# A decode layer on one core: the last 16 columns of wo's last rows as eight small transfers of their own

## The chip, the cores and the metric

The kernel runs on one core of a Trainium2 chip. The core has five engines with queues of their own: TensorE (PE, matmuls and the loads of their weights), VectorE (DVE), ScalarE (ACT), GpSimd (POOL) and SyncE (SP, which issues most transfers). Data move between the chip's main memory (HBM) and the on-chip memory (128 partitions) through 16 transfer (DMA) engines, which all queues share. A transfer is issued by one engine's queue, is cut into packets for the 16 transfer engines, and raises a semaphore when it has landed; whoever needs the data waits until that semaphore has 16.

The metric is the device time of one execution in microseconds (us), lower is better, as the median of several runs.

## What is computed

One token goes through an attention block and a feed-forward block in parallel, and both are added to the input. Cut to what matters:

```python
D, Hq, Hkv, Sk, Dh, F, W = 1024, 32, 4, 65536, 128, 3584, 4096
x  = A_x                                   # 1 x 1024, bf16 as all inputs
xn = layernorm(x)
# attention over the last W = 4096 positions, 8 query heads share a key head
q  = (xn @ wq).reshape(Hq, Dh)             # wq 1024 x 4096
p  = softmax(q . k_cache[:, -W:] * Dh ** -0.5)
o  = p . v_cache[:, -W:]                   # 32 heads x 128 = 4096 numbers
a  = o @ wo                                # wo 4096 x 1024
# feed-forward, with a second layernorm
h  = gelu(layernorm(xn) @ w1 + b1)         # w1 1024 x 3584
b  = h @ w2 + b2                           # w2 3584 x 1024
out = x + a + b
```

Weights and cache together are 40 MB, each byte of which is used once.

## The kernel before

The program is written out by hand, engine by engine; no scheduler reorders it, so the order of each queue is the order of the code.

SP issues all large transfers in one sequence: wq in four pieces (L183), w1 in four (L184), the keys and the values in four pieces each (L185 to L194). Then it waits until the product with w1 is done, since w2 takes w1's place in the on-chip memory and wo takes wq's (tile WA), and issues w2 in four pieces and wo in seven (L285 to L287). The helper `load_rows` (L135) issues such a sequence; its transfers all carry the line L138. At the end SP waits for ScalarE's copy of the result, issues the store of the output (L458) and waits for its landing.

ScalarE issues four small loads at the start: x twice, b2 and b1.

Of wo, partition p holds rows 32p to 32p + 31 of the 4096, one after another, 1024 columns (2 KB) each. So "row c" below means 128 rows of wo, one in each partition, 256 KB in all. `WO_CHUNKS` (L25) says how many of these rows go into each transfer: 8, 8, 8, 4, 2, 1, 1. Each transfer has a semaphore, s_wo0 to s_wo6.

TensorE computes, in this order: the layernorms' sums, the product with wq, the turning of q into columns, the product with w1, the transposes of the keys (L343) with the gelu's part among them, the scores (L365), the softmax's small products, the first chunk of w2, the product with the values (L432), the rest of w2 with the attention output's turning (L443) in between, and at last the seven chunks of wo. The products with w2 and wo are made by `out_rows_mms` (L403): it waits for the chunk's semaphore and then makes four matmuls per row c, one for each quarter of the 1024 output columns. All add into one accumulator. The last matmul raises PE's semaphore, ScalarE copies the result to ORow (L456), and the store follows.

Two things of the code matter for the end of the program: the wo chunks are waited for one by one, in the order of their issue, and the last chunk is a single row c, so that only four matmuls are left when it lands.

Of the kernel before, what the change touches and what calls it, by code (L numbers as in the profile page):

```python
# [9 lines left out]
D = 1024  # L10
# [11 lines left out]
WQ_CHUNKS = [2, 2, 2, 2]  # L22
W1_CHUNKS = [2, 2, 2, 2]
W2_CHUNKS = [9, 9, 8, 2]
WO_CHUNKS = [8, 8, 8, 4, 2, 1, 1]  # L25
PAD = 32


# [12 lines left out]
def bass_parallel_sum__sliding_block_cached__mixer_channel_mlp__decode_kernel(  # L41
# [18 lines left out]
    pe, dve, act, pool, sp = nc.tensor, nc.vector, nc.scalar, nc.gpsimd, nc.sync  # L60

    def sems(name, n):
        return [nc.alloc_semaphore(f"{name}{i}") for i in range(n)]
# [4 lines left out]
    s_k = sems("s_k", HKV)  # L68
    s_v = sems("s_v", HKV)
    s_wo = sems("s_wo", len(WO_CHUNKS))  # L70
    s_w2 = sems("s_w2", len(W2_CHUNKS))

    PE = Track(nc, "S_PE")
# [4 lines left out]
    def sb(name, shape, d):  # L78
        return nc.alloc_sbuf_tensor(name, shape, d)
# [24 lines left out]
    GT = sb("GT", [128, FC + PAD], bf16)  # L104
# [8 lines left out]
    OT = sb("OT", [128, 32 + PAD], bf16)  # L113
# [4 lines left out]
    W2 = W1[:, 0:FC * D]  # L118
    WA = sb("WA", [128, KC * NQ], bf16)
# [10 lines left out]
    wo_p = A_wo.rearrange("(p j) n -> p j n", j=32)  # L130
# [4 lines left out]
    def load_rows(dst, src, chunks, width, semaphores):  # L135
        c0 = 0
        for j, n in enumerate(chunks):
            sp.dma_start(  # L138
                dst[:, c0 * width:(c0 + n) * width].rearrange("p (c n) -> p c n", c=n),
                src[:, c0:c0 + n, :],  # L140
            ).then_inc(semaphores[j], 16)
            c0 += n
# [128 lines left out]
    for h in range(HQ):  # L271
        last = pe.matmul(PSb[:, 7 * 1024 + 2 * h: 7 * 1024 + 2 * h + 1], lhsT=Qrow[0:1, h * 128:(h + 1) * 128],  # L272
                         rhs=identb[0:1, 0:1], is_transpose=True)
# [10 lines left out]

    sp.wait_ge(PE.sem, C["h"])  # L285
    load_rows(W2, w2_p, W2_CHUNKS, D, s_w2)
    load_rows(WA, wo_p, WO_CHUNKS, D, s_wo)  # L287


    KPAIRS = [[0, 1], [2, 3], [4, 5]]  # L290
# [36 lines left out]
    for u in range(NUNIT):  # L327
# [13 lines left out]
        for bb in range(16):  # L341
            o = banks[bb // 8] * 1024 + (bb % 8) * 128
            last = pe.matmul(PSb[:, o:o + 128], lhsT=KT[:, col + bb * 128: col + (bb + 1) * 128],  # L343
                             rhs=identb[:, :], is_transpose=True)
# [16 lines left out]
    for g in range(HKV):  # L361
        if g == HKV - 1:
            wait_kt(pe, 7)
        for b in range(NBLK):
            last = pe.matmul(  # L365
                PS[:, g * 256 + b * 8: g * 256 + (b + 1) * 8],
                lhsT=KT[:, g * W + b * 128: g * W + (b + 1) * 128], rhs=QT[:, g * 8:(g + 1) * 8])
# [32 lines left out]
    def acc(a):  # L400
        return PS[32 * a:32 * a + 32, 6 * 512:6 * 512 + 256]

    def out_rows_mms(weights, vec, chunks, semaphores, j, stop_at=None):  # L403
        c0 = sum(chunks[:j])
        pe.wait_ge(semaphores[j], 16)
        for c in range(c0, c0 + chunks[j]):
            for a in range(4):
                ins = pe.matmul(acc(a), lhsT=vec[:, c:c + 32],  # L408
                                rhs=weights[:, c * D + a * 256: c * D + (a + 1) * 256],
                                start=False, stop=(c == stop_at))  # L410
        return ins
# [4 lines left out]
    for a in range(4):  # L416
        pe.matmul(acc(a), lhsT=identb[0:1, 0:32], rhs=XBR[0:1, a * 256:(a + 1) * 256], start=True, stop=False)
        pe.matmul(acc(a), lhsT=identb[0:1, 0:32], rhs=XBR[0:1, D + a * 256:D + (a + 1) * 256], start=False, stop=False)
    pe.wait_ge(DVE.sem, C["d_GT"])
    out_rows_mms(W2, GT, W2_CHUNKS, s_w2, 0)  # L420
    pe.wait_ge(DVE.sem, C["sump"])
    C["tot"] = PE.mark(pe.matmul(PS[:, 3 * 512:3 * 512 + 1], lhsT=SUMP[:, :], rhs=onesf[:, 0:1]))
    dve.wait_ge(PE.sem, C["tot"])
# [4 lines left out]
    for g in range(HKV):  # L428
        pe.wait_ge(s_v[g], 16)
        for b in range(NBLK):  # L430
            i = g * NBLK + b
            last = pe.matmul(PS[32 * g:32 * g + 32, 4 * 512:4 * 512 + DH],  # L432
                             lhsT=Pb[:, i * REP:i * REP + 32], rhs=V[:, i * DH:(i + 1) * DH],
                             start=(b == 0), stop=(b == NBLK - 1))
# [2 lines left out]
    dve.wait_ge(DVE.sem, C["rec"])  # L437
    C["on"] = DVE.mark(dve.tensor_scalar(out=ON[:, :], in0=PS[:, 4 * 512:4 * 512 + DH], scalar1=REC[:, 0:1],
                                         scalar2=None, op0=ALU.mult))
    out_rows_mms(W2, GT, W2_CHUNKS, s_w2, 1)  # L440
    pe.wait_ge(DVE.sem, C["on"])
    for dq in range(4):
        last = pe.matmul(PS[:, 5 * 512:5 * 512 + 32], lhsT=E4[:, dq * 128:(dq + 1) * 128],  # L443
                         rhs=ON[:, dq * 32:(dq + 1) * 32], start=(dq == 0), stop=(dq == 3))
# [1 line left out]
    dve.wait_ge(PE.sem, C["o2"])  # L446
    C["OT"] = DVE.mark(dve.tensor_copy(OT[:, 0:32], PS[:, 5 * 512:5 * 512 + 32]))
    for j in range(2, len(W2_CHUNKS)):
        out_rows_mms(W2, GT, W2_CHUNKS, s_w2, j)
    pe.wait_ge(DVE.sem, C["OT"])  # L450
    for j in range(len(WO_CHUNKS)):
        last = out_rows_mms(WA, OT, WO_CHUNKS, s_wo, j, stop_at=31)
    C["fin"] = PE.mark(last)

    act.wait_ge(PE.sem, C["fin"])
# [34 lines left out]
```

## Time and profile before

| | |
|---|---|
| median of 3 runs | 102.17 us (101.99 to 102.3) |
| span of the profiled execution, first to last instruction | 100.8 us |
| PE busy, of the span | 69% |
| DVE, ACT, POOL busy | 21%, 14%, 5% |
| read from HBM | 39.86 MB, 395 GB/s over the span |
| DMA packets | 4194, of them 726 under 512 bytes |
| mean granted TensorE clock | 0.823 |

The profile is one execution, taken by the hardware profiler. Its span runs from the program's first to its last instruction. The profiled execution's whole time is not given beside it; the runs' median lies 1.3 to 1.4 us above the span, which is what a launch adds outside of it.

The page's strip divides the span into 40 slices of 2.5 us and gives the busy share of each in tenths. The chain of waits follows the work that ended last back to its beginning. The timeline lists instructions in order of time, alike ones merged, with the idle time before them and what ended it. Windows give the busy times in a chosen stretch; their DMA share is the mean over the 16 transfer engines, so that 1.0 is all sixteen busy (a little over 1 can come up, since packets overlap). The queue table counts packets: q1 is SP's queue, q10 ScalarE's, q8 brings instructions. Every transfer engine that takes part in a transfer has data packets and one 4-byte packet, which raises the semaphore by one.

### The profile page before, as it was taken

Reading aid. Unit: us, or ns where it says so; the run is one execution under the profiler, and the core shown is the slowest. Engines: PE = TensorE matmul, PEld = TensorE weight load, DVE = VectorE, ACT = ScalarE, POOL = GpSimd, SP = SyncE. Lnnn points to the kernel's source line nnn. Section 1 sums busy time; section 2 is a strip of 40 time slices with the busy share of each in tenths; the row PEclk is TensorE's granted clock in tenths of the full one; section 3 lists DMA queues with packets and bytes.
Section 4 is the critical chain, followed back from the end, with each engine's and each line's share of the span. In section 5 each row is a group of like instructions: output and inputs, shape, how many; then the busy total and the mean of one; then the engine's idle time right before and its main releaser. Section 6 shows DMA issues by size and latency. Waiting matters only on the chain.

```text
span 100.8 us, 1803 instructions
## 1 busy us (share of the span) xinstructions
PE 69.3 (69%) x825; PEld 42.7 (42%) x825; DVE 21.4 (21%) x46; ACT 13.8 (14%) x16; POOL 4.8 (5%) x18
## 2 busy tenths in 40 slices
PE   0002399999946999996799984649999934070781
PEld 0001233333304223331799984236999823040420
DVE  0003520000054000002876934555000200000000
ACT  0400060000051000002554740040000000000001
POOL 6740000000000000000000000000000000000000
PEclk9999999999996559999999997555559999555555
DMA  4899999999999999999999999999999999999930
GB/s 104 358 442 432 417 436 416 416 431 427 449 432 392 450 427 404 416 416 426 419 423 423 416 431 456 431 395 443 425 398 447 429 423 435 416 422 403 388 139 1
DMA packets 4194, 39.96 MB, mean 396 GB/s; under 512 B 726, under 2 KB 730, under 8 KB 1244
## 3 DMA queue, kind: packets, MB, share of 16 engines
q1 hardware_dynamic: 3896, 39.85, 94.2%
q8 instruction: 6, 0.10, 0.4%
q10 hardware_dynamic: 292, 0.01, 0.2%
HBM read 39.86 MB, written 0.00 MB: 395 GB/s over the span
## 4 chain that ended last, share of the span: by engine, by line
DMA 38%; PE 34%; SPq 20%; DVE 5%; issue 1%; ACT 1%
PE PS L254 31%; DMA WA<-in_A_wo_dram 30%; SPq L138 20%; DMA XB<-in_A_x_dram 7%; DVE ROW L264 2%; PE PS L272 1%; PE PS L234 1%; PE PS L217 1%; PE PS L408 0%; ACT ORow L456 0%; DVE XNT L225 0%; ACT msx L221 0%; DVE msx L198 0%; DVE msy L198 0%; DVE YT L230 0%
## 5 line engine op out<-in xcount | busy, mean ns | idle before, releaser
L254 PE MATMUL PS<-WA,XNTb 128*1 128x512 bf16 x64 | 16.4, 424 | 0.3 <-DVE msy L198 0.3
L254 PE MATMUL PS<-W,YTb 128*1 128x512 bf16 x56 | 15.0, 438 | 0.0
L408 PE MATMUL PS<-WA,OT 128*32 128x256 bf16 x128 | 7.3, 379 | 9.9 <-DMA WA<-in_A_wo_dram 9.9
L254 PEld LDWEIGHTS PS<-WA,XNTb 128*1 128x1 bf16 x64 | 5.8, 91 | 10.5 <-issue 3.5
L408 PEld LDWEIGHTS PS<-WA,OT 128*32 128x32 bf16 x128 | 3.8, 123 | 13.4 <-DMA WA<-in_A_wo_dram 10.3
L432 PE MATMUL PS<-KV,Pb 128*32 128x128 bf16 x128 | 9.2, 260 | 0.0
L254 PEld LDWEIGHTS PS<-W,YTb 128*1 128x1 bf16 x56 | 5.2, 94 | 9.4 <-issue 4.1
L432 PEld LDWEIGHTS PS<-KV,Pb 128*32 128x32 bf16 x128 | 9.1, 119 | 0.0
L343 PE MATMUL PS<-identb,KV 128*128 128x128 bf16 x128 | 7.5, 219 | 1.5 <-ACT ROW L280 1.5
L343 PEld LDWEIGHTS PS<-identb,KV 128*128 128x128 bf16 x128 | 7.1, 98 | 2.0 <-ACT ROW L280 2.0
L217 PE MATMUL PS<-XT,onesf 128*128 128x16 f32 x2 | 0.6, 384 | 8.7 <-DVE XT L213 8.7
L350 DVE COPY KV<-PS 128x1024 bf16<-128x1024 bf16 x10 | 6.3, 684 | 0.7 <-PE PS L343 0.7
L355 ACT ACTIVATE KV<-PS 128x1024 bf16<-128x1024 bf16 x6 | 5.8, 1018 | 1.9 <-PE PS L343 1.9
L408 PE MATMUL PS<-W,GT 128*32 128x256 bf16 x112 | 4.8, 320 | 1.7 <-DMA W<-in_B_w_dram 1.7
L264 DVE CAST ROW<-PS 1x2048 bf16<-1x2048 f32 x1 | 2.3, 2278 | 15.1 <-PE PS L254 15.1
L282 DVE CAST ROW<-PS 1x2048 bf16<-1x2048 f32 x1 | 2.3, 2279 | 14.8 <-PE PS L254 14.8
L456 ACT ACTIVATE ORow<-PS 128x256 bf16<-128x256 f32 x1 | 0.4, 383 | 31.5 <-PE PS L408 31.5
L408 PEld LDWEIGHTS PS<-W,GT 128*32 128x32 bf16 x112 | 3.5, 111 | 2.5 <-DVE PS L386 2.2
L217 PEld LDWEIGHTS PS<-XT,onesf 128*128 128x128 f32 x2 | 0.5, 310 | 8.7 <-DVE XT L213 8.7
L266 ACT ACTIVATE ROW<-PS 1x2048 bf16<-1x2048 f32 x1 | 1.9, 1866 | 14.1 <-PE PS L254 14.1
L280 ACT ACTIVATE ROW<-PS 1x1536 bf16<-1x1536 f32 x1 | 1.4, 1439 | 16.5 <-PE PS L254 16.5
L365 PE MATMUL PS<-QT,KV 128*128 128x8 bf16 x128 | 3.4, 166 | 0.4 <-DVE KV L350 0.4
(75 smaller groups left out, 34.5 us busy)
## 6 DMA issues: line engine op xcount, KB each, us to landing
WA<-in_A_wq_dram SPq DMA_DIRECT2D x4, 2048.0 KB, 14.1
W<-in_B_w_dram SPq DMA_DIRECT2D x4, 1792.0 KB, 30.6
WA<-in_A_wo_dram SPq DMA_DIRECT2D x3, 2048.0 KB, 38.9
W<-in_B_w_dram SPq DMA_DIRECT2D x2, 2304.0 KB, 22.3
KV<-in_A_k_cache_dram SPq DMA_DIRECT2D x4, 1024.0 KB, 39.4
KV<-in_A_v_cache_dram SPq DMA_DIRECT2D x4, 1024.0 KB, 34.4
W<-in_B_w_dram SPq DMA_DIRECT2D x1, 2048.0 KB, 29.3
WA<-in_A_wo_dram SPq DMA_DIRECT2D x1, 1024.0 KB, 42.2
```

Source lines behind the costliest of these rows:

```text
L138: sp.dma_start(dst[:, c0 * width:(c0 + n) * width].rearrange("p (c n) -> p c n", c=n), src[:, c0:c0 + n, :],).then_inc(semaphores[j], 16)
L217: C["sum1"] = PE.mark(pe.matmul(PS[:, 7 * 512: 7 * 512 + 16], lhsT=onesf[:, :], rhs=XT16[:, 0:16]))
L254: last = pe.matmul(PS[0:1, t * 512:(t + 1) * 512], lhsT=vec[:, k:k + 1], rhs=weights[:, k * width + t * 512: k * width + (t + 1) * 512], s ...
L264: C["d_qrow"] = DVE.mark(dve.tensor_copy(Qrow[:, 0:2048], PS[0:1, 0:2048]))
L266: C["a_qrow"] = ACT.mark(act.activation(out=Qrow[:, 2048:4096], in_=PS[0:1, 2048:4096], func=ACTF.Copy))
L282: C["d_hrow"] = DVE.mark(dve.tensor_copy(Hrow[:, 1536:F], PS[0:1, 1536:F]))
L343: last = pe.matmul(PSb[:, o:o + 128], lhsT=KT[:, col + bb * 128: col + (bb + 1) * 128], rhs=identb[:, :], is_transpose=True)
L350: C["dkt"][u] = DVE.mark(dve.tensor_copy(KT[:, col + 1024 * s: col + 1024 * (s + 1)], PSb[:, bk * 1024:(bk + 1) * 1024]))
L355: C["akt"][u] = ACT.mark(act.activation(out=KT[:, col + 1024: col + 2048], in_=PSb[:, bk * 1024:(bk + 1) * 1024], func=ACTF.Copy))
L365: last = pe.matmul(PS[:, g * 256 + b * 8: g * 256 + (b + 1) * 8], lhsT=KT[:, g * W + b * 128: g * W + (b + 1) * 128], rhs=QT[:, g * 8:(g + ...
L408: ins = pe.matmul(acc(a), lhsT=vec[:, c:c + 32], rhs=weights[:, c * D + a * 256: c * D + (a + 1) * 256], start=False, stop=(c == stop_at))
L432: last = pe.matmul(PS[32 * g:32 * g + 32, 4 * 512:4 * 512 + DH], lhsT=Pb[:, i * REP:i * REP + 32], rhs=V[:, i * DH:(i + 1) * DH], start=(b ...
```

## The change

The wo transfers of 4 and 1 rows become one of 5, so that the chunks are 8, 8, 8, 5, 2, 1. Row 31, the last, is loaded without its last 16 columns (1008 of 1024) by one transfer. These 16 columns, 32 bytes in each of 128 partitions, are loaded by eight transfers of 65, 22, 10, 9, 7, 6, 5 and 4 partitions, issued by SP after it, each with a semaphore of its own (s_tail0 to s_tail7). The last chunk's four matmuls wait for nine semaphores instead of one. What is computed, and the order of the matmuls, stay the same.

```diff
-WO_CHUNKS = [8, 8, 8, 4, 2, 1, 1]
+WO_CHUNKS = [8, 8, 8, 5, 2, 1]
+TAIL_ROWS = [65, 22, 10, 9, 7, 6, 5, 4]
+TAIL_COLS = 16
...
+    s_tail = sems("s_tail", len(TAIL_ROWS))
...
     sp.wait_ge(PE.sem, C["h"])
     load_rows(W2, w2_p, W2_CHUNKS, D, s_w2)
-    load_rows(WA, wo_p, WO_CHUNKS, D, s_wo)
+    load_rows(WA, wo_p, WO_CHUNKS[:-1], D, s_wo)
+    edge = D - TAIL_COLS
+    sp.dma_start(WA[:, 31 * D:31 * D + edge], wo_p[:, 31, 0:edge]).then_inc(s_wo[-1], 16)
+    p0 = 0
+    with nc.allow_non_contiguous_dma(reason="last columns"):
+        for j, n in enumerate(TAIL_ROWS):
+            sp.dma_start(WA[p0:p0 + n, 31 * D + edge:32 * D], wo_p[p0:p0 + n, 31, edge:D]).then_inc(s_tail[j], 16)
+            p0 += n
...
+    w2_done = [[s] for s in s_w2]
+    wo_done = [[s] for s in s_wo[:-1]] + [[s_wo[-1]] + s_tail]
+
     def out_rows_mms(weights, vec, chunks, semaphores, j, stop_at=None):
         c0 = sum(chunks[:j])
-        pe.wait_ge(semaphores[j], 16)
+        for sem in semaphores[j]:
+            pe.wait_ge(sem, 16)
         for c in range(c0, c0 + chunks[j]):
...
-        last = out_rows_mms(WA, OT, WO_CHUNKS, s_wo, j, stop_at=31)
+        last = out_rows_mms(WA, OT, WO_CHUNKS, wo_done, j, stop_at=31)
```

The calls for w2 take `w2_done` in place of `s_w2`, which is the same one semaphore per chunk.

More of the change, by code (lines that the diff above doesn't have):

```diff
@@ L419, in bass_parallel_sum__sliding_block_cached__mixer_channel_mlp__decode_kernel @@
     pe.wait_ge(DVE.sem, C["d_GT"])
-    out_rows_mms(W2, GT, W2_CHUNKS, s_w2, 0)
+    out_rows_mms(W2, GT, W2_CHUNKS, w2_done, 0)
     pe.wait_ge(DVE.sem, C["sump"])
@@ L439, in bass_parallel_sum__sliding_block_cached__mixer_channel_mlp__decode_kernel @@
                                          scalar2=None, op0=ALU.mult))
-    out_rows_mms(W2, GT, W2_CHUNKS, s_w2, 1)
+    out_rows_mms(W2, GT, W2_CHUNKS, w2_done, 1)
     pe.wait_ge(DVE.sem, C["on"])
@@ L448, in bass_parallel_sum__sliding_block_cached__mixer_channel_mlp__decode_kernel @@
     for j in range(2, len(W2_CHUNKS)):
-        out_rows_mms(W2, GT, W2_CHUNKS, s_w2, j)
+        out_rows_mms(W2, GT, W2_CHUNKS, w2_done, j)
     pe.wait_ge(DVE.sem, C["OT"])
     for j in range(len(WO_CHUNKS)):
-        last = out_rows_mms(WA, OT, WO_CHUNKS, s_wo, j, stop_at=31)
+        last = out_rows_mms(WA, OT, WO_CHUNKS, wo_done, j, stop_at=31)
     C["fin"] = PE.mark(last)
```

## The prediction

> **What bounds the kernel now.** I read the strip of the page first, then the end of the chain of waits, then TensorE's timeline there, then the same microseconds in narrow windows.
>
> ```profile
> span 100.8 us, 1803 instructions
> DMA  4899999999999999999999999999999999999930
> ```
>
> The transfer engines are full from slice 3 to slice 38: the kernel is a stream of 40 MB, and compute hides under it. Only the start and the last 5 us are not streaming. The chain of waits (start, length, what) ends so:
>
> ```profile
> 67.91 30.32 DMA WA<-in_A_wo_dram
> 98.24 0.04 issue
> 98.28 0.43 PE PS L408 x3
> 98.74 0.38 ACT ORow L456
> ```
>
> The end is set by the landing of the last wo transfer at 98.24. After it come one weight load and four matmuls (0.43), the copy to ORow (0.38), and the store of the output, issued at 99.15 and landed at 100.79. Nothing in that tail of 2.6 us is touched. TensorE only follows the landings:
>
> ```profile
> 95.74 1.04 PE L408 MATMUL PS<-WA,OT 128*32 128x256 bf16 x16 [0.59 <-DMA WA<-in_A_wo_dram]
> 97.00 1.06 PE L408 MATMUL PS<-WA,OT 128*32 128x256 bf16 x12 [0.22 <-DMA WA<-in_A_wo_dram]
> 98.28 0.41 PE L408 MATMUL PS<-WA,OT 128*32 128x256 bf16 x4 [0.23 <-DMA WA<-in_A_wo_dram]
> ```
>
> Now narrow windows (columns: stretch, length, busy time of five engines, granted clock, DMA share, GB/s):
>
> ```profile
> 95.50:96.00 0.50, 0.26 (x8) 0.21 (x12) 0.00 (x0) 0.00 (x0) 0.00 (x0) 0.50 1.08 414
> 96.30:96.90 0.60, 0.48 (x12) 0.00 (x0) 0.00 (x0) 0.00 (x0) 0.00 (x0) 0.50 0.39 150
> 97.00:97.30 0.30, 0.30 (x8) 0.13 (x8) 0.00 (x0) 0.00 (x0) 0.00 (x0) 0.50 0.39 150
> 97.55:97.85 0.30, 0.27 (x8) 0.11 (x4) 0.00 (x0) 0.00 (x0) 0.00 (x0) 0.50 0.12 41
> ```
>
> From 96.3 to 97.3 the share stands at 0.39, and 6/16 is 0.375: ten transfer engines are done and six still work. The trace's semaphore increments (one per engine and transfer) say it exactly: for the last wo transfer ten arrive from 96.43 to 96.83, six at 97.91, 98.05, 98.10, 98.10, 98.23 and 98.24. What made six late stands in the queue table:
>
> ```profile
> q1 hardware_dynamic: 3896, 39.85, 94.2%
> q8 instruction: 6, 0.10, 0.4%
> q10 hardware_dynamic: 292, 0.01, 0.2%
> ```
>
> Six packets of 16 KB brought instructions, at 35.0, 54.3, 62.5, 73.2, 80.6 and 87.5 us. 0.4% of 16 engines' 100.8 us is 6.45 us, so 1.07 us each, where a 16 KB data packet takes 0.61; after each, one more of the 16 increments of every transfer is some 1.3 us late. Six late engines are left at the end. So an early engine has up to 1.41 us to spare (98.24 - 96.83), a late one none: what the tail transfers cost depends on which engines they load.
>
> **The change, part by part.**
>
> *Merged chunk (4 and 1 rows become 5).* Rows land 0.63 us apart (two rows from 95.74 to 97.00), so five rows are there at 96.37. Sixteen matmuls take 1.04, thirty-two take 1.90 (timeline from 93.25), hence 0.054 more for each; twenty need 1.26 and end at 97.63. The next two rows land when row 31 lands now (work starts at 97.64); eight matmuls take 0.61 and end at 98.25, before the last row's at 98.28. Cost 0, with 0.03 of cover; were it gone, those hundredths would be the price. One transfer less saves each engine a 4-byte semaphore packet, 9 ns plus 6 to the next.
>
> *The last row narrowed to 1008 columns.* A 2048-byte packet takes 84 ns and a 4096-byte one 159, so 32 bytes less save 1.2 ns, eight times on each engine: 0.01. Both savings together: -0.02.
>
> *Eight tail issues on SP.* Issues that don't wait take 0.24 (b2's row, one row) to 0.65 (a wq transfer); eight make 1.9 to 5.2 us. SP ends its last issue at 72.30 now (67.91 plus 4.39) and next has to issue the store at 99.15: 77.5 at worst, covered by 21 us. Without that cover they would add their length.
>
> *Tail packets.* 128 rows of 32 bytes and their semaphore packets follow the last main transfer in the same queue. Sixteen-byte packets (x) took 9 ns and 56-byte ones (b1) 11; the 512-byte rows of the store 28 to 34. Rows show 128 partitions on 16 engines (16 increments each) and the store's 4 rows on 4 (4 data and 4 semaphore packets: 3896 is 27 x 144 + 8). The fullest engine gets at least 5 of 65 rows, 2 of 22 and one of each of the others: 13 packets and 8 semaphore packets. At 10 ns and 15 ns (9 plus the gap) that is 0.25; at the store's 34 ns, 0.56; the other bound, all 128 rows on one engine, is 1.4. On an early engine 0.25 to 0.56 hides in the 1.41. On a late one it adds in full, and an engine with no tail row adds nothing. The trace doesn't name the late engines. With six of sixteen late, I take the slowest to have a middling share, 9 rows and 4 semaphores: 9 x 0.012 + 4 x 0.015 = 0.17.
>
> The Trainium skill, "DMA: Bandwidth & Descriptors", section "Why a DMA increments its semaphore by 16 and not by 1", says that a transfer uses the largest number of engines up to 16 that divides its slowest dimension, the lowest-numbered ones. By that the rows go over 13, 11, 10, 9, 7, 6, 5 and 4 engines: 13 packets and 8 semaphores on the four lowest, 5 and 1 on numbers 11 and 12, none on 13 to 15, so the sum would lie between +0.36 and +0 with the late engine's number. Its section "Rules for kernel authors" speaks against the change: transfers under 64 KB are mostly overhead, to be merged; at the page's fixed 2.0 us each, one after another, eight would cost 16 us. The row that bears on it: the last two one-row transfers, 256 KB each, land 0.64 apart on every engine (97.60 and 98.24), which is 8 x 0.080 and no fixed cost between, so I take packets, not 2 us.
>
> *Nine semaphores before the last weight load* instead of one. One rides on the instruction; eight need extra wait instructions. In the trace such an instruction carries one or two semaphores, takes 51 ns when met, and the weight load starts 76 ns after it (83.444 to 83.520). Four make between 0 (the last to land is the one on the weight load) and 0.29 (the first of the four is the last met: 0.06 + 3 x 0.076). Middle: 0.18. Behind them in the queue stand only the last four matmuls, for which ScalarE's copy waits, and SP's store behind that; all move by the same amount.
>
> Sum: -0.02 + 0.17 + 0.18 = +0.33. The span of 100.83 becomes 101.16; the median of the runs lies 1.34 above the profiled span, so 102.17 becomes **102.50**, within 102.15 and 102.95 (-0.02, and 0.56 + 0.29 - 0.02 = +0.83).
>
> **The rivals.**
>
> *The late engines carry few tail rows.* Then the tail is done while they still move main rows, and at most one late wait remains: -0.02 to +0.08, time **102.2**. For it: ten engines have 1.4 us to spare; against it: nothing says which.
>
> *Semaphores one after another* (slower). If each tail transfer's increment must be confirmed before the next can start, an engine pays 0.33 (store: packet at 100.42, increment at 100.75) to 0.48 us (sem packets of the last wo transfer against their increments) for each of up to eight: 2.6 to 3.8 us on an early engine, less the 1.41; a late one with four pays 1.3 to 1.9. Time about **104.0**. It decides from 1.41 / 8 = 0.18 us per transfer. Against it: a data packet starts 6 ns after each semaphore packet, and no pause shows in the 0.64.
>
> *Tail issues come late* (slower). SP has to wait for room in its queue:
>
> ```profile
> 55.66 0.43 SPq L138
> 56.13 11.73 SPq L138
> ```
>
> The 27th transfer's issue ended at 72.30, when the 18th had landed (72.33): some nine fit. If a tiny transfer takes a full place, the 34th needs the 25th landed (97.6), and from issue to landing the store took 1.64: 99.24, +1.0, time **103.2**. Against it: space counted in packets makes the eight worth 21 packets on the fullest engine, 2.3 transfers of 9.
>
> *Another placing of the instruction packets* (faster). The six late increments spread from 97.91 to 98.24; should the six fall on engines whose stream is ahead, the end comes up to 0.33 earlier: **101.85**. For it: nothing in the kernel fixes the engine. Against it: TensorE's program is the same up to the last waits, so the fetches should come at the same points.
>
> **How the numbers follow.** Below 0.3% (0.31 us) a measurement of this kernel can't be told from no change. Forecast 0.48, and as its sum lies just at that bound I put 0.35 of it above and 0.13 within. Few rows on late engines 0.17, within. Serial semaphores 0.12, late issues 0.08, both slower. Other placing 0.15, of which 0.14 faster. Faster 0.14, same 0.31, slower 0.55. The range of 8 in 10: 101.9 leaves out some 0.08 of the fast case, 103.6 the serial one: 0.12. The likeliest case's own range is 102.15 to 102.95.
>
> **What would show it.** q1 should have 3896 - 144 + 128 packets plus the tail's semaphore packets, 8 at least, and the more the wider each tail transfer spreads. By the skill's rule on divisors it would be 65 exactly, 3945 in all. The last increment of the main last transfer should lie at 98.22, the tails' increments within 0.5 us after their engine's main one; the last weight load then starts up to 0.3 us after the last landing instead of 0.04. SP's last tail issue should end before 80 us. Packets of 32 bytes much over 34 ns, steps of 0.3 us between an engine's tail increments, an SP issue after 90 us, or a seventh instruction packet would make the prediction wrong.

## The result, and the profile after

| | before | after |
|---|---|---|
| median of 4 runs each | 102.15 us (101.99 to 102.3) | 103.69 us (103.46 to 103.8) |
| span of the profiled execution | 100.8 us | 102.1 us (its run: 103.46 us) |

The change makes the kernel slower: the ratio is 1.0143, 95% interval 1.0125 to 1.0160, 1.5 us. The direction was forecast; the size was four to five times the +0.33 of the prediction, and the time lies outside its range. In the profile 1.3 us of the loss shows; the profiled execution was the fastest of the four.

The end of the chain of waits of the changed kernel (start, length, what):

```profile
75.19 23.93 DMA WA<-in_A_wo_dram
99.11 0.49 issue
99.60 0.43 PE PS L422 x4
100.03 0.02 issue
100.05 0.38 ACT ORow L470
```

Two pieces grew. The last landing is at 99.11 instead of 98.24 (+0.87), and it is that of a tail transfer, issued at 75.19. Between it and the matmuls stands 0.49 of "issue" instead of 0.04 (+0.45). What follows has its old lengths. Narrow windows after the main transfer's last packets (stretch, length, busy time of five engines, granted clock, DMA share, GB/s):

```profile
96.40:96.90 0.50, 0.50 (x16) 0.34 (x12) 0.00 (x0) 0.00 (x0) 0.00 (x0) 0.50 0.37 147
97.35:97.70 0.35, 0.35 (x10) 0.14 (x8) 0.00 (x0) 0.00 (x0) 0.00 (x0) 0.50 0.23 51
97.70:99.10 1.40, 0.42 (x8) 0.00 (x0) 0.00 (x0) 0.00 (x0) 0.00 (x0) 0.50 0.00 0
```

The first line is much as before: six of sixteen engines at work, 0.37. The third is the finding. From 97.70 on no packet moves at all, and the last landing comes 1.4 us later. The tail's packets are not slow (each took 9 ns, one every 6 ns, the last at 97.67): what is late is the semaphores. The trace's increments, one per transfer engine and transfer, fall into chains; the two latest are

```
main     tail0  tail1  tail2  tail3  tail4  tail5
97.86    98.05  98.25  98.44  98.65  98.86  99.06
98.11    98.31  98.51  98.70  98.91  99.11
```

(the main increments at the head of the rows are the ones that the spacing fits; the records don't name engines). Each increment comes 0.19 to 0.21 after the one before, whether the transfer gave the engine five packets or one. The early engines' increments follow each other from 96.45 on in steps of some 0.16 to 0.21, and their last one is at 98.17.

The queue table confirms how the tail was spread:

```profile
q1 hardware_dynamic: 3945, 39.85, 92.8%
q8 instruction: 6, 0.10, 0.4%
```

3945 is 3896 - 144 + 128 + 65, so the eight tails took 65 increments; by semaphore they are 13, 11, 10, 9, 7, 6, 5 and 4. That is what the Trainium skill's rule in "DMA: Bandwidth & Descriptors", section "Why a DMA increments its semaphore by 16 and not by 1", gives. With its "lowest-numbered" the two chains above belong to engines 5 and 6: both are in the transfer over 7 engines, one of them in that over 6, none in that over 5. Six of tail0's increments lie at 98.05 or later, so here all late engines had tail rows.

The 0.49 of issue is TensorE's wait instructions. The trace has four, with two semaphores each, at 99.141, 99.281, 99.387 and 99.493, and the weight load at 99.570: 0.14, 0.106, 0.106 and 0.077 from each to what comes next. The last semaphore met stood in the first of the four.

### The profile page after: what moved, and what is told of

It is laid out like the page before. It is cut to its first block, busy times and chain, and to the rows that moved or that the text cites. A ratio compares the mean times of both kernels' runs of the same rounds, so it can differ in the third digit from the quotient of the medians.

```text
span 102.1 us, 1814 instructions
## 1 busy us (share of the span) xinstructions
PE 66.8 (65%) x825; PEld 41.5 (41%) x825; DVE 21.8 (21%) x46; ACT 13.8 (14%) x16; POOL 4.8 (5%) x18
## 3 DMA queue, kind: packets, MB, share of 16 engines
q1 hardware_dynamic: 3945, 39.85, 92.8%
## 4 chain that ended last, share of the span: by engine, by line
DMA 59%; SPq 33%; PE 4%; issue 2%; ACT 0%
DMA W<-in_B_w_dram 36%; DMA WA<-in_A_wo_dram 23%; SPq L141 14%; SPq L292 11%; SPq L296 7%; PE PS L257 3%; PE PS L422 0%; ACT ORow L470 0%
## 5 line engine op out<-in xcount | busy, mean ns | idle before, releaser
L422 PE MATMUL PS<-WA,OT 128*32 128x256 bf16 x128 | 8.0, 416 | 11.9 <-DMA WA<-in_A_wo_dram 11.9
L257 PE MATMUL PS<-W,YTb 128*1 128x512 bf16 x56 | 12.6, 379 | 1.6 <-DMA W<-in_B_w_dram 1.6
L422 PEld LDWEIGHTS PS<-WA,OT 128*32 128x32 bf16 x128 | 4.3, 135 | 15.5 <-DMA WA<-in_A_wo_dram 9.0
L446 PE MATMUL PS<-KV,Pb 128*32 128x128 bf16 x128 | 8.3, 246 | 0.0
L257 PEld LDWEIGHTS PS<-W,YTb 128*1 128x1 bf16 x56 | 4.5, 84 | 9.3 <-DMA W<-in_B_w_dram 2.6
L446 PEld LDWEIGHTS PS<-KV,Pb 128*32 128x32 bf16 x128 | 8.2, 111 | 0.0
L375 PEld LDWEIGHTS PS<-QT,KV 128*128 128x128 bf16 x128 | 3.3, 96 | 0.6 <-DVE KV L360 0.6
```

The source lines that it names most:

```text
L257: last = pe.matmul(PS[0:1, t * 512:(t + 1) * 512], lhsT=vec[:, k:k + 1], rhs=weights[:, k * width + t * 512: k * width + (t + 1) * 512], s ...
L375: last = pe.matmul(PS[:, g * 256 + b * 8: g * 256 + (b + 1) * 8], lhsT=KT[:, g * W + b * 128: g * W + (b + 1) * 128], rhs=QT[:, g * 8:(g + ...
L422: ins = pe.matmul(acc(a), lhsT=vec[:, c:c + 32], rhs=weights[:, c * D + a * 256: c * D + (a + 1) * 256], start=False, stop=(c == stop_at))
```

## The experiments

The runs' numbers are ratios to the kernel before, run on the same chip beside them; its median was 102.25 to 102.29 there.

**Is the merge free?** The kernel before with one line changed.

```diff
-WO_CHUNKS = [8, 8, 8, 4, 2, 1, 1]
+WO_CHUNKS = [8, 8, 8, 5, 2, 1]
```

> The kernel before with chunks 8, 8, 8, 5, 2, 1 and nothing else of the change. Theory (what the tail transfers cost is one step of about 0.2 us for each semaphore increment behind another on the same transfer engine, plus the wait instructions): the merge is free, 102.15 within 0.15. Rival (the merged chunk makes TensorE late for the last row): the last weight load starts well after the last landing, 102.4 or more.

Measured 1.0003 (0.9993 to 1.0013). The merge costs nothing; the weight load of the last row starts 0.04 behind its landing (98.57 to 98.61) as before. The chain of this execution shows how little was to spare:

```profile
96.71 0.04 issue
96.75 1.85 PE PS L408 x25
98.60 0.02 issue
98.61 0.44 PE PS L408 x3
```

From the landing of the five rows on TensorE works without a break, and it is through just when the last row's weight load may start.

**One tail transfer instead of eight.**

```diff
-TAIL_ROWS = [65, 22, 10, 9, 7, 6, 5, 4]
+TAIL_ROWS = [128]
```

> The changed kernel with all 128 rows of the 16 columns in one transfer: 8 packets and one increment on each of 16 engines, two semaphores to wait for. Theory (a step of 0.2 us per increment, whatever the rows): one step and one wait instruction, 0.2 + 0.1, so 102.45. Rival (the small packets cost, as the slowest engine had 10 of them in the changed kernel and has 8 here): four fifths of the 0.87 us by which the last landing moved, and 0.1, so 102.95.

Measured 1.0011 (0.9998 to 1.0024), 0.1 us, less than either theory said. The chain:

```profile
67.87 30.36 DMA WA<-in_A_wo_dram
98.23 0.14 issue
98.37 0.43 PE PS L422 x4
```

The tail lands 0.15 behind the main row (98.08 to 98.23), and one wait instruction adds 0.1. The main row itself landed earlier than in the profile of before, within what executions differ by. Eight packets per engine are nearly free, against the rival. Three of the ten runs lie apart, at 102.61 to 102.63; the profiled one (102.22) is not among them, so what they waited for isn't known.

**Three tail transfers.**

```diff
-TAIL_ROWS = [65, 22, 10, 9, 7, 6, 5, 4]
+TAIL_ROWS = [65, 33, 30]
```

> The changed kernel with three tail transfers of 65, 33 and 30 rows, which by the divisors go over 13, 11 and 15 transfer engines: three increments behind the main one on engines 5 and 6, where the changed kernel has six and five. Theory (0.19 to 0.2 us a step on a late engine): the last landing at 98.7 to 98.9, two wait instructions, 0.5 to 0.7 over the kernel before. Rival (rows count, not transfers): as many rows on the engines as in the changed kernel, so 1.1 or more.

Measured 1.0040 (1.0025 to 1.0055), 0.4 us, under the 0.5 to 0.7 of the theory and far from the rival's 1.1. The last landing is at 98.78, and the chain that ends there is 98.38, 98.58, 98.78: steps of 0.20 for the same number of rows in fewer transfers.

**Eight tail transfers over all engines.**

```diff
-TAIL_ROWS = [65, 22, 10, 9, 7, 6, 5, 4]
+TAIL_ROWS = [16] * 8
```

> The changed kernel with tail transfers of 16 rows each: every transfer engine has 8 packets and 8 increments. Theory (0.19 to 0.2 us for each increment behind another): the last landing is 8 steps after the last main one, 98.1 + 1.55 = 99.65, and as the last to land is in the last wait instruction, the weight load starts 0.1 later; 1.6 us over the kernel before. Rival (small packets): 8 packets where the slowest engine had 10, a last landing near 98.9, and 0.8 over the kernel before.

Measured 1.0141 (1.0124 to 1.0157), 1.4 us.

```profile
76.45 23.25 DMA WA<-in_A_wo_dram
99.69 0.14 issue
99.83 0.43 PE PS L422 x4
```

The last landing is at 99.69, where the theory put 99.65; the main row's last is at 98.42, so eight steps took 1.27, 0.16 each. The last data packet had ended at 98.07, 1.6 us before the last landing. Fewer packets on the slowest engine than in the changed kernel (8 against 10) and a later end: not packets but transfers count. And issue is 0.14 here, because the last to land stood in the last of the four wait instructions. The step is somewhat shorter with one packet in each transfer on every engine; why it is 0.16 here and 0.20 there stays open.

**Wider tail rows.**

```diff
-TAIL_COLS = 16
+TAIL_COLS = 256
```

> The changed kernel with 256 columns (512 bytes a row) in the tail instead of 16. Theory (steps per increment, whatever the bytes): main rows end 0.15 earlier, five or six steps of 0.2, wait instructions as before; last landing 98.9 to 99.2, 1.4 us over the kernel before. Rival (packets under 512 bytes are what is slow): the steps shrink to the packets' 0.03 to 0.14, and it is 0.6 or less over the kernel before.

Measured 1.0071 (1.0038 to 1.0103), but the ten runs form two groups: five at 102.52 to 102.58 and five at 103.38 to 103.62. The profiled run is of the higher group (103.38). There the steps are as before with 16 times the bytes (98.76, 98.96 and 99.17 at the end), so the theory holds for it and the small size of the packets isn't the cause. The lower group has no profile. That its late engines are ones with few tail rows would explain it, but this isn't shown; the expectation's 1.4 holds for half the runs only (1.2).

**Eight tails on engines that are early.**

```diff
-TAIL_ROWS = [65, 22, 10, 9, 7, 6, 5, 4]
+TAIL_ROWS = [25, 25, 25, 25, 17, 5, 4, 2]
```

> The changed kernel with tail transfers of 25, 25, 25, 25, 17, 5, 4 and 2 rows, which by the divisors go over 5, 5, 5, 5, 1, 5, 4 and 2 transfer engines, the lowest-numbered: eight increments still on the lowest engine, none on any above number 4. Theory (the loss is increments behind one another on an engine that an instruction packet had made late): where numbers 0 to 4 are early, their eight steps end with the late engines' main row at 98.2 to 98.5, and it is 0.2 to 0.6 over the kernel before. Rival (eight small transfers cost what they cost, wherever they go): 1.5 over the kernel before.

Measured 1.0002 (0.9992 to 1.0012): nothing is left of the loss.

```profile
90.17 8.02 DMA WA<-in_A_wo_dram
98.18 0.14 issue
98.32 0.43 PE PS L422 x3
```

Eight transfers, nine semaphores, and up to eight increments one after another, but all on engines that were early: no chain among them is late. They run from 96.44 to 98.18, while the late engines finish the main row at 98.11. The longest is eight steps of 0.18 behind a main increment at 96.75. Eight increments in a row, which cost up to 1.5 us elsewhere, lie here in the 1.4 us that the early engines have to spare. SP issued the last of these transfers only at 90.17, and still in time; the issue next after that of the 17 rows, which go over one engine, had taken 8.50 us, presumably for want of room in that engine's queue. The theory's bound of 0.2 was even too high.

**One semaphore for all.** The nine transfers raise one semaphore, waited for once at 144.

```diff
...
-            sp.dma_start(WA[p0:p0 + n, 31 * D + edge:32 * D], wo_p[p0:p0 + n, 31, edge:D]).then_inc(s_tail[j], 16)
+            sp.dma_start(WA[p0:p0 + n, 31 * D + edge:32 * D], wo_p[p0:p0 + n, 31, edge:D]).then_inc(s_wo[-1], 16)
...
-    wo_done = [[s] for s in s_wo[:-1]] + [[s_wo[-1]] + s_tail]
+    wo_done = [[s] for s in s_wo]
...
-        for sem in semaphores[j]:
-            pe.wait_ge(sem, 16)
+            pe.wait_ge(sem, 16 * (1 + len(TAIL_ROWS)) if sem is s_wo[-1] else 16)
```

> The changed kernel, its nine transfers of the last row raising one semaphore that is waited for once at 144. Theory: the last landing stays where it is (99.1 in the profile) and the wait instructions' 0.42 us goes, so 103.25. Rival (the nine waits are most of the loss): 102.5 or less.

Measured 1.0082 (1.0065 to 1.0099), 0.85 us, where the theory's 103.25 meant 1.1.

```profile
99.40 0.04 issue
99.45 0.43 PE PS L421 x4
```

Issue is back at 0.04, so the waits' 0.4 is gone; the late landing stays, 99.40 in this execution, the slowest of its four (103.34). The waits are the smaller part, and the rival falls.

**The changed kernel again**, unaltered.

> The changed kernel unaltered, beside the others on one chip. Theory: 1.5 us over the kernel before, of which about 0.4 is wait instructions after the last landing and the rest the last landing itself. Rival (the size of the loss hangs on the chip): another number.

Measured 1.0118 (1.0098 to 1.0139), 1.2 us, with runs from 103.32 to 103.66 on this chip. In its profile the last landing is at 99.39 and the weight load at 99.77; two of six late engines have no tail0 increment (only four of those lie at 98.02 or later). So which engines are late differs between executions. The last landing belongs to six steps behind a main increment at 98.19, where the first profile has six behind 97.86 and five behind 98.11: so the time at which such an engine ends its main row counts too. Whether the difference to the first 1.0143 is of that kind or the chip's wasn't told apart.

**Tails in the middle of the stream.** The eight are issued ahead of wo's first transfer.

```diff
     load_rows(W2, w2_p, W2_CHUNKS, D, s_w2)
-    load_rows(WA, wo_p, WO_CHUNKS[:-1], D, s_wo)
     edge = D - TAIL_COLS
-    sp.dma_start(WA[:, 31 * D:31 * D + edge], wo_p[:, 31, 0:edge]).then_inc(s_wo[-1], 16)
     p0 = 0
...
             p0 += n
+    load_rows(WA, wo_p, WO_CHUNKS[:-1], D, s_wo)
+    sp.dma_start(WA[:, 31 * D:31 * D + edge], wo_p[:, 31, 0:edge]).then_inc(s_wo[-1], 16)
```

> The changed kernel with the eight tail transfers issued ahead of wo's first one, in the middle of the stream, so that they have long landed at the end. Theory: a tail's increment is held until the writes before it are confirmed, while data behind it go on; then nothing is left at the end but nine waits that are met early, 102.2. Rival (the whole queue of an engine stops at each increment, data too): engines 5 and 6, late by an instruction packet, lose another 5 or 6 times 0.2, so 103.2 or more.

Measured 1.0009 (0.9999 to 1.0019). The steps are there all the same: one chain of increments reads 78.42, 78.62, 78.83, 79.04, 79.24, 79.45. But the data behind them go on: the last landing of all is at 98.35, where six steps of held data would have made 99.4. Not all goes on: the last early engine ends at 97.45 instead of 96.83, 0.6 of the 1.6 us that eight steps take, which the early engines can afford.

**A version meant to beat both.** 640 columns of row 27 go to the five lowest engines, well ahead of the end.

```diff
...
+    for p0, p1, a, b in ((0, 128, 24 * D, cut), (0, 125, cut, end), (125, 128, cut, end)):
+        sp.dma_start(WA[p0:p1, a:b], wo_f[p0:p1, a:b]).then_inc(s_wo[3], 16)
...
```

The three transfers raise one semaphore, waited for at 48; the other wo transfers stay as they were.

> The kernel before, with 640 columns of row 27 (1280 bytes) taken out of the transfer of four rows and loaded by one of 125 rows (5 transfer engines by the divisors) and one of 3, both early enough to have landed before the end. Theory (the end is set by engines that an instruction packet delayed, and numbers 0 to 4 are not among them): late engines save 8 x 1280 bytes, 0.37 us, and the lowest five gain 25 packets, 0.9 net of that, which fits into their 1.3 to 1.4 to spare: 0.2 to 0.4 under the kernel before. Rival (the late engines fall anywhere, or extra packets slow all): no change or 0.5 and more over it.

Measured 1.0046 (1.0028 to 1.0065): slower by 0.5 us, a miss. The same stretch in windows, first of this kernel, then of before:

```profile
94.00:94.50 0.50, 0.50 (x16) 0.40 (x12) 0.00 (x0) 0.00 (x0) 0.00 (x0) 0.50 1.02 269
94.50:95.00 0.50, 0.50 (x16) 0.35 (x12) 0.00 (x0) 0.00 (x0) 0.00 (x0) 0.50 1.02 264
```

```profile
94.00:94.50 0.50, 0.50 (x16) 0.33 (x12) 0.00 (x0) 0.00 (x0) 0.00 (x0) 0.50 1.02 418
94.50:95.00 0.50, 0.50 (x14) 0.16 (x4) 0.00 (x0) 0.00 (x0) 0.00 (x0) 0.50 0.94 373
```

All sixteen are busy in both, but move a third less while the transfer of 125 rows is under way. A packet of 6912 bytes took some 264 ns before it and mostly 383 to 401 beside it. It slows the other engines' packets too; what they contend for wasn't tried. The early engines' spare time is real, but a transfer of this shape can't collect it.

## Why the prediction was wrong

- *What bounds the kernel.* Right: the last landing on engines that an instruction packet made late. The experiment with low engines shows it best, and every profile has the six packets.
- *Merge, narrowed row, SP's issues.* Right in effect: 1.0003 for the merge, though nothing was left of its cover, and SP's last tail issue ended at 77.6, a little past the prediction's upper end of 77.5 and far ahead of the store.
- *Tail packets, +0.17.* Here the forecast failed. The packets were over-priced, if anything (6 ns apart, not 10 to 15), but a semaphore packet was priced at 15 ns, by the gap to the next data packet. On engines 5 and 6 an increment follows the one before by 0.19 to 0.21 us in the changed kernel. The term measured +0.87: five steps behind 98.11, or six behind 97.86, where the last main increment of before was at 98.24. (By its own terms, -0.02, 0.25 and 0.18, the upper end of the sum by divisors is +0.41 and not +0.36.)
- *Nine semaphores, +0.18, at most 0.29.* Mis-sized: +0.42 to the weight load in the profile. From one wait instruction to the next it took 0.106, after the first 0.14; the 0.076 of the forecast is the time from a wait instruction to a weight load, and that is 0.077 here too. The last semaphore met stood in the first instruction, the worst place.
- *The rival "semaphores one after another"* was the mechanism, and its 104.0 the nearest number; it got 0.12. Its price of 0.33 to 0.48 was the time from packet to increment of a single transfer, twice the step. Its condition, 0.18 per transfer on early engines, was met only just: the early engines' last increment was at 98.17, and late ones set the end.
- *The argument against that rival was false.* That a data packet starts 6 ns after each semaphore packet, and that no pause shows in 0.64, tells that data aren't held, which the tails in mid-stream confirm for the most part. It tells nothing of increments that would come closer than 0.2 us, since SP's last transfers were 0.64 apart. The profile of before had the step all the same, at its start: between 7.37 and 7.71 the sixteen semaphore packets of the first wq transfer and the sixteen of x's transfer on ScalarE's queue lie in pairs 6 ns apart, and their increments come at 7.72 to 8.05 and at 7.93 to 8.22, some 0.2 apart. The records don't name the engines, so it is a hint and no proof, but one that speaks for the rival.
- *Few tail rows on late engines*, 102.2: not so in the profiled executions; it may be the lower group of the wider tail, unshown. *Late issues*: no. *Another placing of the instruction packets*: the placing does vary between executions, but no gain came of it.
- *The sum against the time.* Profile to profile +1.32 (0.87 to the landing, 0.45 from there to the first matmul), medians +1.54; the rest is that the profiled execution was the fastest of its four. That the direction was right is in part luck: the larger part of the loss came in the way that the prediction argued against.

## What to carry to other kernels

At the end of a stream count the semaphore increments that each transfer engine has to make, not the packets: several short transfers in a row end some 0.2 us apart on the same engine here, however small they are, and the engine that is late already pays in full. No cost was measured where the stream goes on behind (1.0009), or where only early engines take part (1.0002). Waiting for many semaphores cost TensorE about 0.1 us for each pair behind the last one met; one shared semaphore with the full count takes that away.

## What the runs showed of the hardware

- Each instruction packet of 16 KB delays one transfer engine by some 1.3 us for the rest of the program, a different engine each of the six times: in the profile of before one increment of a transfer is late behind the first packet (37.21, the others by 35.79), and six are at the end (97.91 to 98.24, the others by 96.83). Which engines differs between executions: numbered as in the section on the result they are 5 and 6 with four of the engines 9 to 15 in both profiles of the changed kernel, once all six among the lowest 13, once four.
- A transfer of 125 rows over 5 engines slowed the others' packets by some 45% (264 to about 388 ns for 6912 bytes, in one profile).
